# Attention with squared Relu, then a gated feed-forward block: transposes and some output tiles on all 128 rows of TensorE

## The chip, the core and the metric

The kernel runs on one core of a Trainium2 chip. The metric is the device time of one execution in microseconds (us): 432.54 before the change, the median of 7 runs (431.4 to 437.14). Inputs and output are float32 in HBM; the loads turn them to bfloat16 on the way, and all matmuls take bfloat16 and add up in float32.

## The reference

Batch 8, 12 heads, 448 tokens, 64 numbers per head. The attention has no softmax; its output, heads side by side (768 wide), goes through a gated feed-forward block with 1536 inner columns.

```python
scores = scale * np.matmul(q, k.transpose(0, 1, 3, 2))        # scale = 1/sqrt(64)
attn = np.maximum(scores, 0.0) ** 2 / S                       # S = 448
x = np.matmul(attn, v)                                        # then heads side by side: (8*448, 768)
g = x @ w_gate
gelu = 0.5 * g * (1.0 + erf(g * inv_sqrt2))
out = (gelu * (x @ w_val)) @ w_out
```

## The kernel before, in words

**Four quarters.** TensorE's array of 128 rows and 128 columns is used as four tiles of 64x64. `mm` (L158) takes a row half and a column half. A sum over 128 rows is done as two sums over 64 rows, by the lower row half (row 0) and the upper one (row 1), into the same PSUM bank. The two halves may not write a bank at the same time, so the upper half's part of a bank runs after the lower half's part: `then` (L307) puts it into the order behind it, at least 0.3 us of planned work later, and `wait_lower` (L162) makes it wait. While the upper half works on one bank, the lower half works on the next. Work whose halves write different banks runs side by side: `both` (L301).

**Stages.** A batch passes through these:
- *Transposes.* Scores need queries and keys with the 64 numbers of a head on the partitions. Queries of a chunk of 64 tokens lie on partitions 0 to 63, keys on 64 to 127 (`qk16`, 7 chunks a head). For batches 0 and 1 (`EARLY` = 2) TensorE transposes them (`add_transposes`, L319, matmuls on L333): 28 for a pair of heads, with queries on the lower and keys on the upper rows, into separate banks or halves, and VectorE copies each to `qkT` (L339). Batches 2 to 7 are transposed by DMA (`add_dma_transposes`, L248): VectorE regroups four heads (L258, into `qkr`, which has one buffer), then SP issues two transposing DMAs (L262).
- *Scores* (`add_scores`, L361): 21 units a batch. ScalarE takes the Relu out of PSUM (L387), VectorE squares it (L393).
- *Values* (`add_values`, L419): attention times v for a pair of heads; VectorE scales the bank into `xT` (L443).
- *Gate and value* (`add_gate_value`, L464): for each of 12 chunks of 128 inner columns one bank for the gate (6 steps on each row half), taken out by ScalarE as Gelu (L482), and one for the value, multiplied by VectorE into `uT` (L487).
- *Output* (`add_out`, L512): 28 tiles of 128 tokens, each in two banks of 384 columns (the last tile in three of 384, 192 and 192), 12 steps on each row half. ScalarE copies the bank to `osb` (L538); SP, at the end ScalarE too, issues the stores (L543).

PSUM has two slots for scores and transposes of batch 1 (`psS`) and a ring of four banks for the rest (`psF`).

**What sets the order.** The kernel writes every instruction in an order that a small planner (`run_plan`, L23) works out when it is built. Every piece of work gets a planned time `at` (from L561 on). The gate, value and output work of the batches stands in a row; batch 0 has output tiles 0 and 1 behind it, batch 1 has tiles 2 to 5, and so on, batch 7 tiles 23 to 27. The attention of batch 0 is placed ahead of time 0; that of batch 1 between `LO1` (L609) and 6 us before batch 1's gates start; that of later batches beside the feed-forward work of the batch before them. In planned time the gates of batch 0 take 0 to 27.2, tile 0 27.2 to 31.1, tile 1 31.1 to 35.0; batch 1's gates end at 62.2, tile 2 takes 62.2 to 66.1, and the scores of batch 2 take 41 to 71.8.

`lower`, sorted by `at`, is the fixed order of the lower rows (PE0). The upper rows' operations are sorted by the planned time of the lower operation beside which, or behind which, they belong; the planner takes from this list (PE1) the first that can start. The instruction stream of TensorE is the two merged by planned start, and it runs in that order. VectorE, ScalarE and SP take their operations in the order in which the planner finds them ready, with a planned arrival for every load; an `IDLE` operation of 2.0 us puts a regrouping behind the planned arrival of its loads. In gaps of the plan ahead of time `FILL`, `fill` (L284) puts matmuls on a zero tile.

Of the kernel before, what the change touches and what calls it, by code (L numbers as in the profile page):

```python
# [88 lines left out]
def kernel(  # L89
# [10 lines left out]
    nc = tc.nc  # L100
# [6 lines left out]
    P = 64  # L107
# [13 lines left out]
    WOG = 3  # L121
    SB = 2
    FB = 4
    FILL = 64.0
    EARLY = 2

    out_scale = 1.0 / (D * S)
# [115 lines left out]
    def by_group(t):  # L243
        return t.rearrange("d (m c r) x -> d m c r x", m=NM, c=SC)
# [3 lines left out]
    def add_dma_transposes(b, m):  # L248


        wait = Op("IDLE", 2.0, lambda: None,
                  [head_op[b, pr, i] for pr in (2 * m, 2 * m + 1) for i in range(2)])
        IDLE.append(wait)

        def emit_copy():
            if b not in qkr:
                qkr[b] = lpool.tile([128, NM, SC, 4, D], bf16, name="qkr", tag="qkr")
            nc.vector.tensor_copy(  # L258
                qkr[b][:, m], qk16[b].rearrange("p (h c d) -> p c h d", c=SC, d=D)[:, :, 4 * m:4 * m + 4])

        def emit_transpose(c0, c1):
            nc.sync.dma_start_transpose(  # L262
                by_group(qkT_tile(b))[:, m, c0:c1].rearrange("d c r x -> d (c r) x"),
                qkr[b][:, m, c0:c1].rearrange("p c h d -> p (c h d)"))

        copy = Op("DVE", 0.65, emit_copy, [wait, *tr_op.get((b - 1, m), ())], lag=0.15, prio=3)
        DVE.append(copy)
        tr_op[b, m] = [Op("SP", 0.19 * 2 * (c1 - c0), lambda c0=c0, c1=c1: emit_transpose(c0, c1),
                          [copy, last_s.get(b - 2)], lag=4.5) for c0, c1 in ((0, VC), (VC, SC))]
        SP.extend(tr_op[b, m])  # L270
# [13 lines left out]
    def fill(t0, t1):  # L284

        reader = in_bank[-FB] if len(in_bank) >= FB else None
        if reader is not None:
            if reader.end is None:
                return
            t0 = max(t0, reader.end + 0.2)  # L290
        n = int((t1 - t0 - 0.15) / 0.115)
        if t1 > FILL or n < 1:
            return
        t = new_bank(None)
        for _ in range(n):
            nc.tensor.matmul(t[:, 0:256], warm[:, 0:128], warm[:, 0:256], start=True, stop=True)  # L296

    def ring_dep():
        return [ring[-FB]] if len(ring) >= FB else []
# [19 lines left out]
    def add_transposes(at, b, m, rs):  # L319

        box = {}

        def emit(i, n, c):
            if b and not box:
                t = psS.tile([128, 2, 1024], bf16, name="sp", tag="S")
                for x in range(2):
                    box[x] = t[:, x, 0:len(rs) * SC * P].rearrange("d (r x) -> d r x", r=len(rs))
            elif i not in box:
                box[i] = new_bank(t_op[b, m, rs[0], i], [128, len(rs), SC * P], bf16)
            t = box[i]  # L330
            src = qk16[b].rearrange("p (h c d) -> p h c d", c=SC, d=D)
            for j in range(2):
                nc.tensor.transpose(  # L333
                    t[HALF[j], n, c * P:(c + 1) * P], src[HALF[i], 2 * (2 * m + rs[n]) + j, c, :],
                    ident[HALF[i], HALF[i]], tile_position=(P * i, P * j))

        def emit_copy(i):
            dst = by_group(qkT_tile(b))[:, m].rearrange("d c r x -> d r c x")
            nc.vector.tensor_copy(  # L339
                dst[:, rs[0]:rs[-1] + 1, :, HALF[i]],  # L340
                box[i].rearrange("d r (c p) -> d r c p", c=SC))

        ops = [[], []]
        for i in range(2):
            have = [*(head_op[b, 2 * m + r, i] for r in rs), *(units[-SB:1 - SB] if b else ring_dep())]
            for n in range(len(rs)):
                for c in range(SC):
                    ops[i].append(Op(f"PE{i}", 0.05, lambda i=i, n=n, c=c: emit(i, n, c),
                                     have, lag=0.2))
            t = Op("DVE", 0.07 + 0.235 * len(rs), lambda i=i: emit_copy(i),  # L350
                   [ops[i][-1], last_s.get(b - 2)], lag=0.2, prio=1)
            for r in rs:
                t_op[b, m, r, i] = t
            DVE.append(t)
            if not b:
                ring.append(t)
        if b:
            units.append(t)
        both(at, zip(*ops), GS / 2 if b else 0.0)

    def add_scores(at, b, u):  # L361


        m, w = divmod(u, SC)
        tail = w == VC - 1
        prs = (2 * m, 2 * m + 1) if tail else (2 * m + (w > VC - 1),)
        cl = w if w < VC else w - VC
        box = {}

        def emit(j, pr):  # L370
            if not box:
                box[0] = psS.tile([128, 2, 512], f32, name="sp", tag="S")
            sp = box[0]
            t = by_group(qkT_tile(b))[HALF[j], m, :, pr % 2, :]
            for i in range(2):
                if tail:
                    n0 = (pr % 2) * S // 2
                    qs = t[:, :, i * P // 2:(i + 1) * P // 2]
                    mm(sp[HALF[i], j, n0:n0 + S // 2].rearrange("k (c p) -> k c p", c=SC),
                       t[:, VC - 1, HALF[1]], qs, j, i, True, True)  # L380
                else:
                    mm(sp[HALF[i], j, 0:S].rearrange("k (c p) -> k c p", c=SC),
                       t[:, cl + i * VC, HALF[1]], t[:, :, HALF[0]], j, i, True, True)

        def emit_relu():
            rl = box[1] = rpool.tile([128, 2, S], bf16, name="rl", tag="rl")
            nc.scalar.activation(rl[:, :, :], box[0][:, :, 0:S], AF.Relu)  # L387

        def emit_sq():
            a = apool.tile([128, 2, S], bf16, name="attnT", tag="attnT")  # L390
            for pr in prs:
                att[b, pr, VC - 1 if tail else cl] = a
            nc.vector.tensor_tensor(a[:, :, :], box[1][:, :, :], box[1][:, :, :], op=ALU.mult)  # L393

        if b < EARLY:
            have = [t_op[b, m, pr % 2, i] for pr in prs for i in range(2)]
        else:
            have = tr_op[b, m]
        have = [*have, *units[-SB:1 - SB]]
        ops = [[Op(f"PE{j}", 0.095 if tail else 0.189, lambda j=j, pr=pr: emit(j, pr), have, lag=0.24)  # L400
                for pr in prs] for j in range(2)]
        last_s[b] = ops[1][-1]
        relu = Op("ACT", 0.8, emit_relu, [ops[0][-1], ops[1][-1], *sq_list[-4:-3]], lag=0.18, prio=2)
        n_a = len(sq_list)
        sq = Op("DVE", 0.54, emit_sq, [relu, *att_free[n_a - 12:n_a - 11]] if n_a >= 12 else [relu],
                lag=0.2, prio=2)
        units.append(relu)
        sq_list.append(sq)
        att_free.append(None)
        for pr in prs:  # L410
            sq_op.setdefault((b, pr), []).append((sq, n_a))
            sq_of[b, pr, VC - 1 if tail else cl] = sq
        ACT.append(relu)
        DVE.append(sq)
        both(at, zip(*ops))
# [96 lines left out]
    def add_out(at, t, g):  # L512
# [27 lines left out]
        def emit_store(j, engine, cols):  # L540
# [1 line left out]
            rows = out[b * S:(b + 1) * S, :].rearrange("(p c) d -> c p d", c=SC)  # L542
            engine.dma_start(rows[c, :, cols], osb[t][HALF[j], cols])  # L543

        ops = [[Op(f"PE{r}", step, lambda r=r, fc=fc: emit(r, fc),
                   [wo_op[fc // WOG], *(u_op[b, fc] for b, _ in chunks),
                    *(ring_dep() if r == 0 and fc == 0 else ())], lag=0.24)
                for fc in range(FC)] for r in range(2)]
        cp = Op("ACT", 0.48, emit_copy, [ops[1][-1]], prio=1)
        ring.append(cp)  # L550
        ACT.append(cp)
        if last:
# [2 lines left out]
        elif g == NG - 1:  # L555
            SP.extend(Op("SP", 0.6, lambda j=j: emit_store(j, nc.sync, slice(0, d_model)), [cp], prio=-1)
                      for j in range(2))
        then(at, step, *ops, cp)


    for h0, h1 in ((0, 2), (2, 4), (4, 8), (8, 12)):  # L561
# [44 lines left out]
            tile_no += 1  # L606
    starts.append(at)
    LEAD = 6.0
    LO1 = 2.0  # L609
    for b in range(B):  # L610
        if b == 0:
            lo, hi = -60.0, -12.0
        elif b == 1:
            lo, hi = LO1, starts[1] - LEAD
        elif b == 2:
            lo, hi = starts[1] + 6.0, starts[2] - LEAD
        else:
            lo, hi = starts[b - 1] - LEAD, starts[b] - LEAD
        step = (hi - lo) / NU
        if b < EARLY:  # L620
            for m in range(NM):
                for rs in ((0,), (1,)) if b == m == 0 else ((0, 1),):
                    work.append((lo + SC * m * step - (5.0 if b else 3.0), 1, add_transposes, (b, m, rs)))
        for pr in range(NPAIR):
            u = SC * (pr // 2) + (VC - 1, SC - 1)[pr % 2]
            work.append((lo + u * step + max(4.5, (3.2 if b == 0 else 2.5) * step), 2, add_values, (b, pr)))
        for u in range(NU):
            work.append((lo + u * step, 3, add_scores, (b, u)))
# [83 lines left out]
```

## Time and profile before

| | |
|---|---|
| median of 7 runs | 432.54 us |
| profiled execution: its time, its span | 432.57 us, 430.8 us |
| busy: TensorE, weight loads, ScalarE, VectorE, GpSimd | 419.1, 362.2, 224.7, 211.8, 71.8 us |
| transposes on TensorE (L333) | 336 of 64 columns, 5.6 to 53.9 us |
| fillers (L296) | 39 of 256 columns, the last at 28.6 us |
| regrouping (L258) | 18, 1079 ns each |
| output matmuls (`ff<-wo,uT`) | 2736 recorded, 320 ns of one on average |
| tiles 0 and 1 | 67.4 to about 80 us |
| tiles 23 to 27 | about 404.7 to 426.2 us |

A profile is one execution. The span runs from the first to the last instruction. A matmul's recorded time is from its start until its last result is out; matmuls overlap, so four in four tiles take as long as one, and the distance between starts says what a stream costs. A line of the page's groups or of the timeline gives start, length, engine, line of the kernel, operation, tile written and tiles read, shapes and count; the square brackets say how long the engine was idle before it and what released it. "SPq" and "ACTq" are the queues that issue DMAs.

### The profile page before, as it was taken

Reading aid. Unit: us, or ns where it says so; the run is one execution under the profiler, and the core shown is the slowest. Engines: PE = TensorE matmul, PEld = TensorE weight load, DVE = VectorE, ACT = ScalarE, POOL = GpSimd, SP = SyncE. Lnnn points to the kernel's source line nnn. Section 1 sums busy time; section 2 is a strip of 40 time slices with the busy share of each in tenths; the row PEclk is TensorE's granted clock in tenths of the full one; section 3 lists DMA queues with packets and bytes.
Section 4 is the critical chain, followed back from the end, with each engine's and each line's share of the span. In section 5 each row is a group of like instructions: output and inputs, shape, how many; then the busy total and the mean of one; then the engine's idle time right before and its main releaser. Section 6 shows DMA issues by size and latency. Waiting matters only on the chain.

```text
span 430.8 us, 19964 instructions
## 1 busy us (share of the span) xinstructions
PE 419.1 (97%) x9279; PEld 362.2 (84%) x9279; DVE 211.8 (49%) x345; ACT 224.7 (52%) x323; POOL 71.8 (17%) x117
## 2 busy tenths in 40 slices
PE   8999799989999999999999999999999999999995
PEld 4668599767898888979999978979999988977895
DVE  3966565357534575356633675356633555212200
ACT  3956564366566555555556555555546555322221
POOL 8655420113000230023100131012200000000000
PEclk9999999999999999999999999999999999999999
DMA  8999999999324997269914697359912100220024
GB/s 105 192 199 197 201 208 185 166 140 166 59 76 87 93 166 69 76 102 143 128 40 111 86 150 104 78 81 139 153 40 77 40 4 2 48 68 3 3 76 111
DMA packets 75378, 44.92 MB, mean 104 GB/s; under 512 B 36128, under 2 KB 71840, under 8 KB 75296
## 3 DMA queue, kind: packets, MB, share of 16 engines
q0 software_dynamic: 37088, 24.39, 42.6%
q1 hardware_dynamic: 37968, 19.08, 25.9%
q8 instruction: 72, 1.18, 1.1%
q10 hardware_dynamic: 240, 0.20, 0.2%
q14 instruction: 10, 0.08, 0.1%
HBM read 48.76 MB, written 11.01 MB: 139 GB/s over the span
## 4 chain that ended last, share of the span: by engine, by line
PE 89%; DVE 3%; SPq 2%; DMA 2%; ACT 1%; issue 1%; ACTq 0%; DVEq 0%
PE ff L159 80%; PE sp L159 7%; DMA qkT<-qkr 2%; SPq L262 2%; DVE attnT L393 1%; PE ff L676 1%; ACT rl L387 1%; DVE qkT L339 1%; PE ff L296 1%; SPq L543 1%; PE sp L333 1%; DVE xT L443 0%; ACT osb L538 0%; PE ff L333 0%; ACTq L543 0%
## 5 line engine op out<-in xcount | busy, mean ns | idle before, releaser
L159 PE MATMUL ff<-xT,wg 64*64 64x448 bf16 x2304 | 218.6, 349 | 1.9 <-issue 1.9
L159 PE MATMUL ff<-xT,wv 64*64 64x448 bf16 x2304 | 217.8, 349 | 1.4 <-DVE uT L487 1.3
L387 ACT ACTIVATE rl<-sp 128x896 bf16<-128x896 f32 x168 | 152.1, 919 | 103.1 <-PE sp L159 84.1
L159 PE MATMUL ff<-wo,uT 64*64 64x384 bf16 (+1 forms) x2736 | 151.0, 320 | 0.3 <-issue 0.3
L159 PEld LDWEIGHTS <-wv 64*64 64x64 bf16 x2304 | 126.0, 107 | 18.5 <-issue 3.4
L393 DVE TENSOR_TENSOR attnT<-rl 128x896 bf16<-128x896 bf16 x168 | 103.8, 622 | 74.6 <-ACT rl L387 73.1
L159 PEld LDWEIGHTS <-wg 64*64 64x64 bf16 x2304 | 126.2, 107 | 17.0 <-issue 3.2
L159 PEld LDWEIGHTS <-uT 64*64 64x64 bf16 x2736 | 126.5, 107 | 5.1 <-issue 0.6
L159 PE MATMUL sp<-qkT 64*64 64x448 bf16 (+1 forms) x768 | 107.4, 328 | 1.0 <-ACT rl L387 0.9
L487 DVE TENSOR_TENSOR uT<-gel,ff 128x448 bf16<-128x448 bf16 x96 | 59.5, 620 | 74.4 <-PE ff L159 63.9
L159 PE MATMUL ff<-attnT,v 64*64 64x448 bf16 (+1 forms) x768 | 85.4, 326 | 0.4 <-DVE attnT L393 0.4
L482 ACT ACTIVATE gel<-ff 128x448 bf16<-128x448 f32 x96 | 52.1, 543 | 49.2 <-PE ff L159 48.1
L538 ACT COPY osb<-ff 128x384 f32<-128x384 f32 (+1 forms) x57 | 26.9, 471 | 49.9 <-PE ff L159 46.6
L159 PEld LDWEIGHTS <-qkT 64*64 64x64 bf16 x768 | 43.7, 106 | 8.6 <-issue 3.6
L159 PEld LDWEIGHTS <-v 64*64 64x64 bf16 x768 | 45.3, 107 | 4.9 <-issue 0.6
L443 DVE TENSOR_SCALAR xT<-ff 128x448 bf16<-128x448 f32 x48 | 29.9, 623 | 32.4 <-PE ff L159 30.9
L211 POOL DMA_DIRECT2D qk<-in_q_dram x25 | 15.6, 623 | 157.2 <-DVE uT L487 148.3
L224 POOL DMA_DIRECT2D v<-in_v_dram x44 | 27.4, 629 | 34.3 <-DVE uT L487 25.6
L211 POOL DMA_DIRECT2D qk<-in_k_dram x25 | 15.4, 616 | 37.8 <-DVE uT L487 27.7
L258 DVE COPY qkr<-qk 128x1792 bf16<-128x1792 bf16 x18 | 19.3, 1079 | 3.1 <-DMA qk<-in_k_dram 3.1
L333 PEld LDWEIGHTS <-qk 64*64 64x64 bf16 x336 | 8.9, 112 | 3.9 <-issue 2.5
L333 PE MATMUL sp<-ident,qk 64*64 64x64 bf16 x168 | 6.2, 192 | 0.9 <-DVE qkT L339 0.8
(22 smaller groups left out, 44.4 us busy)
## 6 DMA issues: line engine op xcount, KB each, us to landing
out_dram<-osb SPq DMA_DIRECT2D x54, 192.0 KB, 2.7
v<-in_v_dram POOLq DMA_DIRECT2D x42, 128.0 KB, 6.1
qk<-in_q_dram POOLq DMA_DIRECT2D x23, 224.0 KB, 5.1
qk<-in_k_dram POOLq DMA_DIRECT2D x23, 224.0 KB, 5.7
wg<-in_moe_w_gate_dram POOLq DMA_DIRECT2D x6, 384.0 KB, 10.7
wv<-in_moe_w_val_dram POOLq DMA_DIRECT2D x6, 384.0 KB, 11.7
wo<-in_moe_w_out_dram POOLq DMA_DIRECT2D x4, 576.0 KB, 14.9
v<-in_v_dram POOLq DMA_DIRECT2D x2, 384.0 KB, 11.2
```

The lines of the kernel that those rows point to most:

```text
L159: return nc.tensor.matmul(o, lhsT, rhs, start=start, stop=stop, tile_position=(P * row, P * col))
L211: op = load(4 * (h1 - h0) * S * D, lambda: nc.gpsimd.dma_start(tile_of().rearrange("p (h x) -> p h x", h=H)[:, h0:h1, :], src[b, h0:h1].re ...
L224: return nc.gpsimd.dma_start(v16[b][HALF[i], h0:h1, :, :], v[b, h0:h1].rearrange("h (p c) d -> p h c d", c=SC)[:, :, c0:c0 + VC, :])
L258: nc.vector.tensor_copy(qkr[b][:, m], qk16[b].rearrange("p (h c d) -> p c h d", c=SC, d=D)[:, :, 4 * m:4 * m + 4])
L262: nc.sync.dma_start_transpose(by_group(qkT_tile(b))[:, m, c0:c1].rearrange("d c r x -> d (c r) x"), qkr[b][:, m, c0:c1].rearrange("p c h d ...
L333: nc.tensor.transpose(t[HALF[j], n, c * P:(c + 1) * P], src[HALF[i], 2 * (2 * m + rs[n]) + j, c, :], ident[HALF[i], HALF[i]], tile_positio ...
L387: nc.scalar.activation(rl[:, :, :], box[0][:, :, 0:S], AF.Relu)
L393: nc.vector.tensor_tensor(a[:, :, :], box[1][:, :, :], box[1][:, :, :], op=ALU.mult)
L443: nc.vector.tensor_scalar_mul(xT[b][:, pr, :], box[0][:, 0:S], scalar1=out_scale)
L482: nc.scalar.activation(gel[b, fc][:, :], box[0][:, 0:S], AF.Gelu)
L487: u_op[b, fc].ins = nc.vector.tensor_tensor(uT[b][:, fc, :], gel.pop((b, fc))[:, :], box[0][:, 0:S], op=ALU.mult).ins
L538: nc.scalar.copy(ob[:, cols], box[0][:, 0:N])
```

## The change

- Transposes for batches 0 and 1: one matmul transposes a chunk of queries and keys of one head together, from all 128 rows, with a 128x128 identity as the moving operand (128 columns), to one of two column halves: 14 for a pair of heads. A pair has its own bank (batch 0) or half of a slot (batch 1), one copy on VectorE, and in the plan one lower operation of 0.5 us with an empty upper one beside it.
- Planned times: `FILL` 30 instead of 64, fillers of 512 columns, batch 1's attention from 5.0 (`LO1`) instead of 2.0, other times for the transposes, and for regroupings of batches 3 to 7 an `IDLE` of 5.0 us.
- Output tiles 1, 2 and 23 to 27 ("full") are computed on all 128 rows: each of the 12 steps is two matmuls (one per column half) on 128 rows. In the plan a step is a lower operation with an empty upper one of the same cost beside it (`both`), where the other tiles keep `then`.

```diff
-    FILL = 64.0
+    FILL = 30.0
...
-        wait = Op("IDLE", 2.0, lambda: None,
+        wait = Op("IDLE", 2.0 if b == EARLY else 5.0, lambda: None,
...
-        n = int((t1 - t0 - 0.15) / 0.115)
+        n = int((t1 - t0 - 0.15) / 0.22)
...
-            nc.tensor.matmul(t[:, 0:256], warm[:, 0:128], warm[:, 0:256], start=True, stop=True)
+            nc.tensor.matmul(t[:, :], warm[:, 0:128], warm[:, :], start=True, stop=True)
...
+        def emit(r):
+            if b == 0:
+                t = new_bank(t_op[b, m, r], [128, SC, 2 * P], bf16)
+            else:
+                if not box:
+                    box["S"] = psS.tile([128, 2, 1024], bf16, name="sp", tag="S")
+                t = box["S"][:, r, 0:SC * 2 * P].rearrange("d (c x) -> d c x", c=SC)
+            box[r] = t
             src = qk16[b].rearrange("p (h c d) -> p h c d", c=SC, d=D)
...
+            for c in range(SC):
+                for j in range(2):
+                    nc.tensor.transpose(t[HALF[j], c, :], src[:, 2 * (2 * m + r) + j, c, :],
+                                        ident[:, :], tile_position=(0, P * j))
+
+        def emit_copy(r):
+            nc.vector.tensor_copy(by_group(qkT_tile(b))[:, m, :, r, :], box[r])
+
+        last = units[-SB:1 - SB]
+        for r in rs:
+            have = [*(head_op[b, 2 * m + r, i] for i in range(2)), *(last if b else ring_dep())]
+            lo = Op("PE0", 0.5, lambda r=r: emit(r), have, lag=0.2)
+            hi = Op("PE1", 0.4, lambda: None)
+            hi.after = lo
+            t = t_op[b, m, r] = Op("DVE", 0.54, lambda r=r: emit_copy(r),
+                                   [lo, last_s.get(b - 2)], lag=0.2, prio=1)
             DVE.append(t)
             if not b:
                 ring.append(t)
+            both(at, [(lo, hi)])
...
+        def emit_full(fc):
+            if not box:
+                box[0] = new_bank(cp)
+            i, o = divmod(fc, WOG)
+            for j, (b, c) in enumerate(chunks):
+                nc.tensor.matmul(box[0][HALF[j], 0:N], uT[b][:, fc, c * P:(c + 1) * P],
+                                 wo[i][:, o, cols], start=fc == 0, stop=fc == FC - 1,
+                                 tile_position=(0, P * j))
+
+
+        full = 0 < t < SC // 2 or 2 * t + 2 > SC * (B - 1) - 2
+        if full:
+            ops = [[Op("PE0", step, lambda fc=fc: emit_full(fc),
+                       [wo_op[fc // WOG], *(u_op[b, fc] for b, _ in chunks),
+                        *(ring_dep() if fc == 0 else ())], lag=0.24)
+                    for fc in range(FC)],
+                   [Op("PE1", step, lambda: None) for _ in range(FC)]]
+            for lo, hi in zip(*ops):
+                hi.after = lo
...
-        cp = Op("ACT", 0.48, emit_copy, [ops[1][-1]], prio=1)
+        cp = Op("ACT", 0.48, emit_copy, [ops[0 if full else 1][-1]], prio=1)
...
-        then(at, step, *ops, cp)
+        if full:
+            both(at, zip(*ops), step)
+        else:
+            then(at, step, *ops, cp)
...
-    LO1 = 2.0
+    LO1 = 5.0
...
-                for rs in ((0,), (1,)) if b == m == 0 else ((0, 1),):
-                    work.append((lo + SC * m * step - (5.0 if b else 3.0), 1, add_transposes, (b, m, rs)))
+                for rs in ((0,), (1,)) if b == 0 else ((0, 1),):
+
+                    x = ((0.5 if m else 1.5) * step if rs == (1,) else -4.6) if b == 0 else -5.0 if m else -2.0
+                    work.append((lo + SC * m * step + x, 1, add_transposes, (b, m, rs)))
```

More of the change, by code (lines that the diff above doesn't have):

```diff
@@ L321, in add_transposes @@
         box = {}
[L323 to L330, printed above, removed]
-            src = qk16[b].rearrange("p (h c d) -> p h c d", c=SC, d=D)
[L332 to L353, printed above, removed]
+        def emit(r):
[6 more added lines that the diff above has]
+            box[r] = t
+            src = qk16[b].rearrange("p (h c d) -> p h c d", c=SC, d=D)
+            for c in range(SC):
+                for j in range(2):
+                    nc.tensor.transpose(t[HALF[j], c, :], src[:, 2 * (2 * m + r) + j, c, :],
+                                        ident[:, :], tile_position=(0, P * j))
@@ L356, in add_transposes @@
                 ring.append(t)
+            both(at, [(lo, hi)])
         if b:
             units.append(t)
-        both(at, zip(*ops), GS / 2 if b else 0.0)
     def add_scores(at, b, u):
@@ L395, in add_scores @@
         if b < EARLY:
-            have = [t_op[b, m, pr % 2, i] for pr in prs for i in range(2)]
+            have = [t_op[b, m, pr % 2] for pr in prs]
         else:
@@ L543, in emit_store @@
             engine.dma_start(rows[c, :, cols], osb[t][HALF[j], cols])
-        ops = [[Op(f"PE{r}", step, lambda r=r, fc=fc: emit(r, fc),
+        def emit_full(fc):
[16 more added lines that the diff above has]
+        else:
+            ops = [[Op(f"PE{r}", step, lambda r=r, fc=fc: emit(r, fc),
                    [wo_op[fc // WOG], *(u_op[b, fc] for b, _ in chunks),
@@ L557, in add_out @@
                       for j in range(2))
-        then(at, step, *ops, cp)
+        if full:
+            both(at, zip(*ops), step)
+        else:
+            then(at, step, *ops, cp)
     for h0, h1 in ((0, 2), (2, 4), (4, 8), (8, 12)):
```

## The prediction

> **What bounds the kernel now.** I read the page's summary first, then the busy time by stretches, then the timeline at each stretch in which TensorE is not full, and last the chain of waits.
>
> ```profile
> PE 419.1 (97%) x9279; PEld 362.2 (84%) x9279; DVE 211.8 (49%) x345; ACT 224.7 (52%) x323; POOL 71.8 (17%) x117
> ```
>
> TensorE (PE) is busy for 97% and the others for about half. The stretches (columns: window, its length, then busy time and count for PE, weight loads, DVE, ACT, POOL) say where the other 3% and the hidden losses lie:
>
> ```profile
> 0.00:8.00 8.00, 6.81 (x89) 3.29 (x89) 1.15 (x4) 1.54 (x3) 6.95 (x18) 1.00 0.65 81
> 8.00:28.00 20.00, 18.55 (x401) 11.98 (x393) 17.88 (x33) 17.27 (x21) 12.41 (x19) 1.00 1.36 191
> ...
> 50.50:53.00 2.50, 0.56 (x20) 0.37 (x21) 0.00 (x0) 0.32 (x1) 0.61 (x1) 1.00 1.31 203
> 53.00:90.00 37.00, 36.35 (x797) 31.52 (x793) 20.34 (x32) 18.46 (x27) 5.19 (x8) 1.00 1.20 186
> 90.00:95.00 5.00, 3.71 (x80) 2.67 (x76) 2.42 (x4) 3.27 (x5) 0.61 (x1) 1.00 0.85 113
> 95.00:404.00 309.00, 309.00 (x6856) 272.94 (x6855) 154.92 (x249) 165.25 (x239) 34.27 (x56) 1.00 0.57 84
> ```
>
> From 8 to 28 us VectorE and ScalarE are full: the attention of batch 0 goes through 21 Relu evictions of about 0.83 us. At 50.5 TensorE stands for 1.94 us (in the chain, "issue"): the weights wg of the last two chunks, issued at 39.20 and 12.9 us to landing, land at about 52.1. All loads ahead of them run at 200 GB/s without a pause, so this moment is fixed. From 53 to 404 TensorE is the bound, with one hole:
>
> ```profile
> 93.21 1.09 DVE L258 COPY qkr<-qk 128x1792 bf16<-128x1792 bf16 x1 [1.98 <-DMA qk<-in_k_dram]
> ...
> 94.87 0.38 PE L159 MATMUL ff<-xT,wv 64*64 64x448 bf16 x4 [1.29 <-DVE uT L487]
> ```
>
> VectorE stands 1.98 us on the regrouping copy of batch 3, whose keys have not landed; the uT multiply behind it is late, and TensorE idles 1.29 us for its bank. The last stretch is the end:
>
> ```profile
> 423.86 2.30 PE L159 MATMUL ff<-wo,uT 64*64 64x192 bf16 x45
> ```
>
> ```profile
> 426.44 0.32 ACT L538 COPY osb<-ff 128x192 f32<-128x192 f32 x1 [0.63 <-PE ff L159]
> 426.79 0.50 ACTq L543 DMA_DIRECT2D out_dram<-osb  x1
> 427.32 0.32 ACT L538 COPY osb<-ff 128x192 f32<-128x192 f32 x1 [0.57 <-ACT osb L538]
> ```
>
> The lower rows are out of work at 423.8 and the upper rows, which trail by about one bank, run alone until 426.16. Two banks end almost together, so the last eviction waits behind its neighbour's store issue and starts 1.16 us after the last matmul.
>
> **What the Trainium skill says.** "TensorEngine Tiling (Array Packing)", Key Properties: "Changing tiling mode (not just tile) drains the TensorE". The trace of before has such changes, where a 128x128 filler stands between 64x64 matmuls:
>
> ```profile
> 12.21 0.36 PE L159 MATMUL sp<-qkT 64*64 64x448 bf16 x2
> 12.50 0.10 PEld L296 LDWEIGHTS <-warm 128*128 128x128 bf16 x1 [0.20 <-issue]
> 12.50 0.28 PE L296 MATMUL ff<-warm 128*128 128x256 bf16 x1
> 12.71 0.14 PEld L159 LDWEIGHTS <-v 64*64 64x64 bf16 x4
> 12.72 0.38 PE L159 MATMUL ff<-attnT,v 64*64 64x448 bf16 x2
> ```
>
> 448 columns take 0.187 us (pairs start 0.19 apart), so the first matmul has streamed by 12.40; the filler starts 0.10 later. It streams its 256 columns in 0.11 (fillers in a row: four in 0.61 us, (0.61-0.27)/3), to 12.61, and the next weights start 0.10 later. So the trace agrees: a change costs 0.10 us, there and back 0.20, with the exposed weight load 0.22. "TensorE: Matmul & The Clock Gate" (Part 3, The mechanism) says that a weight load overlaps a running matmul only in other row groups; the warm-up speaks against a cost here: its 20 matmuls on 128 rows take 4.48 us, so 10 pairs step by (4.48-0.63)/9 = 0.43 us, all of it the 512 columns at the cold clock, loads hidden. "PSUM — Partial Sum Buffer" (PSUM bank collisions raise a hardware error) says that row tiles may not write one bank at once: that is why the upper rows trail, and the trace shows the trail at the end.
>
> **The change part by part.** The sum is made against the profiled execution's 432.57 us (span 430.8); the median of the runs is 432.54, the same.
>
> *Transposes.* 336 of 64 columns on quarter arrays become 168 of 128 columns on half arrays. Per pair of heads: before 28 x 64/4 = 448 array columns, 0.19 us; after 14 x 128/2 = 896, 0.37 us. For the six pairs of batch 1 that is +1.1 us, and each of three blocks adds a change of mode there and back, 0.7; the evictions stay the same elements (0.62 us per 128x896). +1.8 us, at nothing, since it lies ahead of 52.1, where TensorE now stands 1.94 us for weights (and about 1 us for earlier weights at 35 to 40). Batch 0's lie under the full ScalarE. If that cover were gone, it would be +1.8. A gain here ends in the same wait.
>
> *LO1 5 instead of 2.* Of batch 1's score units, one more falls behind chunk 10 of the gates, planned at 22.68: before, 2+1.286u < 22.68 holds for u to 16; after, 5+1.143u for u to 15. One unit, +0.19 us behind the fixed moment.
>
> *FILL, coarser fillers.* The last filler runs at 28.6 us, so the limit of 30 cuts nothing; fewer fillers before it leave TensorE idle under the full ScalarE. 0; if TensorE fell back to its cold clock there, it would be part of a second, under the same cover.
>
> *Regrouping 3 us later* (batches 3 on). The copy at 93.21 goes behind about two more multiplies; the 1.98 us wait is gone and with it the idle 1.29. What is late next: two DMA transposes on SP per block, behind any output stores there, but their scores run some 20 us later; nothing. -1.3.
>
> *Full output tiles.* 7 tiles, 24 steps each, of two 384-column matmuls on 128 rows: 24 x 0.16 = 3.84 us, as many as before on four quarters; no gain in streaming. But in the plan a full step is a lower operation and an idle upper one beside it. The trailing upper operations of the bank before are merged with those idle ones one to one. So the stream reads: two full steps, one upper step alone, two full steps, one alone. Each such step costs its own 0.16 to 0.19 us, the lower rows idle, and two changes of mode, 0.22.
> - Tile 1 (now about 71 to 78 us): 12 upper steps of tile 0 and 4 of the last values of batch 1, which the plan puts inside this tile (at 32.4 of 31.1 to 35.0). Some 6 of these find a partner, 10 run alone: 10 x (0.16+0.22) = 3.8, and the lower values' own change 0.22, in all +4.0.
> - Tile 2 (about 112 us): 6 upper steps of the last value chunk, 3 score units of batch 2 and values of one pair (planned between 62.2 and 66.1). The upper halves of the scores come later than the lower ones, so 3+3 excursions, 1 for the values, some 6 alone: 13 x 0.22 = 2.9, and 9 steps alone of 0.18 = 1.6. +4.5.
> - Tiles 23 to 27: 8 upper steps are left when tile 23 starts (gates' matmuls until 405.98 beside outputs from 404.7): 8 x (0.19+0.22) = 3.3. Given back: the 2.4 us of upper rows alone at the end, and 1.1 of the last eviction, since banks now end 0.96 us apart. -0.2.
>
> Sum: +0.2 -1.3 +4.0 +4.5 -0.2 = +7.2. 432.6 + 7.2 = 439.8, say 440.
>
> The price of a change between 64 rows and 128 rows with 64 columns is not in the trace itself; the filler has 128 columns. Bounds: 0 (the rows only have to meet) to 0.15 (the first transposes start about 0.13 after the warm-up has streamed, at the cold clock). I take 0.11, as the drain is of the rows. With 0 the sum loses (10+1+13+8) x 0.22 = 7.0: +0.2.
>
> **The rivals.**
> - *Changing costs nothing* (the other side): full steps wait only for the rows they need. For it: none of the changes seen has the same 64 columns on both sides. Against it: all fillers between 64x64 matmuls show 0.2 us. Place: tiles 1, 2 and 23. It gives 432.8, no change. It decides where a round trip costs below about 0.1 us: there the sum is under +3.5.
> - *The upper rows have caught up ahead of tiles 1 and 2*: then neither is merged, the end gains 2 us and the hole 1.3: 429.3. Against it: the trail of 2.4 us at the end, which nothing shortens between.
> - *Weight loads no longer hidden* in full tiles, for want of other row groups: 7 x 24 steps with up to 0.1 us each, +17 us less half: 448 or more. Against it: the warm-up's 0.43 us.
> - *The cover ahead of 52.1 does not reach*: batch 0 ends later by over 3 us, which comes on top: 443.
>
> **How the numbers follow.** Merged steps with changes of mode 0.58 (436 to 444: a change at 0.06 to 0.15 gives +4 to +10, and some excursions more or less give the rest); changes free 0.22 (431 to 434.5); rows caught up 0.10 (428 to 431); loads exposed or cover gone 0.10. The predicted time is the likeliest's, 440. The range 431 to 444 holds the first two, 0.80, and leaves out the last two. About 1% is what a measurement of this kernel can tell from no change: slower by over 1% is 0.52 of the first and the last 0.10, 0.62; within 1% the rest of the first, the second, and half of the third, 0.33; faster 0.05.
>
> **What would show it.** Right: in the timeline of tiles 1, 2 and 23, 128x64 and 64x64 matmuls alternate, each change with 0.1 us of no start; tile 1's two banks take about 8 us instead of 4; no DVE wait on L258 at 93; the last evictions 0.96 us apart. Wrong: full and half steps following without a gap, or upper steps done ahead of the full tiles. The transposes are wrong if the wait for wg at 52 is gone; the later regrouping if the multiply still waits there.

## The result and the profile after

The changed kernel takes 442.02 us, the median of 12 runs (440.81 to 443.35); the kernel before takes 432.58 in the runs beside it. The ratio is 1.0208 (95% interval 1.0182 to 1.0235): slower by 2.1%. Some executions of one and the same kernel come out over 1.5% slower than its fastest; medians here are of all runs, ratios and their intervals of the faster runs alone. The forecast was 440.0, with 431 to 444 as its range. The profiled execution of the changed kernel took 443.35 us, the slowest of the 12 and 1.3 more than the median, and its span is 441.5, 10.7 longer than that of before.

The page's summary of the changed kernel:

```profile
PE 433.6 (98%) x8729; PEld 350.1 (79%) x8729; DVE 211.3 (48%) x343; ACT 224.5 (51%) x323; POOL 71.6 (16%) x117
```

550 matmuls fewer than before, and TensorE "busy" for 14.5 us longer. A matmul's recorded time is much longer than its streaming (0.35 us where starts lie 0.16 apart), so busy time hides short standstills: the distance between starts has to be read. Before, the matmuls of both row halves run side by side in tile 1, 26 in 1.30 us, four for every 0.16 (timeline of TensorE):

```profile
74.88 1.30 PE L159 MATMUL ff<-wo,uT 64*64 64x384 bf16 x26
```

The timeline in tile 1 of the changed kernel (tile size ahead of the operands):

```profile
72.15 0.35 PE L544 MATMUL ff<-wo,uT 128*64 128x384 bf16 x2
72.43 0.35 PE L159 MATMUL ff<-wo,uT 64*64 64x384 bf16 x2
72.71 0.35 PE L544 MATMUL ff<-wo,uT 128*64 128x384 bf16 x2
73.00 0.35 PE L159 MATMUL ff<-wo,uT 64*64 64x384 bf16 x2
```

Full steps on 128 rows (L544) and single steps of the upper 64 rows (L159) alternate, and the starts lie 0.28 to 0.29 us apart. 384 columns stream in 0.16, so 0.12 goes with each change of the row count here. The weight loads (PEld) of the same stretch start only together with their matmul:

```profile
72.43 0.11 PEld L159 LDWEIGHTS <-uT 64*64 64x64 bf16 x2 [0.17 <-issue]
72.71 0.11 PEld L544 LDWEIGHTS <-uT 128*64 128x64 bf16 x2 [0.17 <-issue]
```

Between full steps in a row the next weights are loaded while the matmul before still runs (in e4's trace 73.70 to 73.81, for a matmul at 73.86). So the price of a change may be an emptied array, a weight load that is not hidden (0.11), or both; no run here separates them.

The same stands at the seam of the last gates with tile 23, now against steps of 448 columns (0.19):

```profile
414.03 0.35 PE L544 MATMUL ff<-wo,uT 128*64 128x384 bf16 x2
414.31 0.38 PE L159 MATMUL ff<-xT,wg 64*64 64x448 bf16 x2
414.62 0.35 PE L544 MATMUL ff<-wo,uT 128*64 128x384 bf16 x2
```

0.28 from full to half, 0.31 back: 0.12 each over the streaming. At every change between 128 and 64 rows in the output tiles, the distance of the starts less the streaming of the first was summed: 34 changes at tile 1 (together 3.83 us), 22 at tile 2 (2.34), 22 at tile 23 (2.39). That is 78 changes, 8.56 us, 0.110 each on average.

The regrouping copy of batch 3, which stood 1.98 us for its load, waits for nothing any more (a line of VectorE's timeline without brackets):

```profile
99.90 1.08 DVE L258 COPY qkr<-qk 128x1792 bf16<-128x1792 bf16 x1
```

At the end the evictions of the last banks start 0.9 us apart, and the last one waits for TensorE, not for its neighbour's store (ScalarE's timeline):

```profile
437.24 0.32 ACT L532 COPY osb<-ff 128x192 f32<-128x192 f32 x1 [0.63 <-PE ff L544]
437.59 0.50 ACTq L537 DMA_DIRECT2D out_dram<-osb  x1
438.13 0.32 ACT L532 COPY osb<-ff 128x192 f32<-128x192 f32 x1 [0.57 <-PE ff L544]
```

Laying the two profiled executions side by side at the uT multiplies (each batch and chunk has one) gives where the time went, in us:

| stretch | predicted | after less before |
|---|---|---|
| to the end of batch 0's gates (transposes, FILL, LO1) | +0.2 | -0.1 |
| tile 1 | +4.0 | +5.9 |
| batch 1, chunks 3 to 6 (the hole at 93) | -1.3 | -1.4 |
| rest of batch 1's chunks | 0 | -0.2 |
| tile 2 | +4.5 | +3.9 |
| batches 2 to 7 | 0 | +1.6 |
| tiles 23 to 27 and the end | -0.2 | +1.1 |
| sum | +7.2 | +10.8 |

Each row is from one execution of either kernel. How far one execution can be trusted shows in the first row: the changed kernel and e1, e4, e5, e6, e7 and e8 below have the same plan up to tile 1, and their profiles stand there at -1.5 to +0.7 us against before (their median is -0.7); e2 and e3, with the order of before, at +0.9 and +0.5.

The 1.6 in batches 2 to 7 is mostly one stop of TensorE:

```profile
272.24 0.35 PE L159 MATMUL ff<-xT,wg 64*64 64x448 bf16 x1
...
273.78 0.35 PE L159 MATMUL ff<-xT,wg 64*64 64x448 bf16 x1 [1.18 <-issue]
```

Of a pair of gate matmuls that normally start together, the second starts 1.5 us later, released by nothing that the profile shows. The kernel before stood in this manner at 50.5 us. The third group of experiments is about it.

### The profile page after: what moved, and what is told of

It reads as the page before. It is cut to its first block, busy times and chain, and to the rows that moved or that the text cites. A ratio compares the mean times of both kernels' runs of the same rounds, so it can differ in the third digit from the quotient of the medians.

```text
span 441.5 us, 18868 instructions
## 1 busy us (share of the span) xinstructions
PE 433.6 (98%) x8729; PEld 350.1 (79%) x8729; DVE 211.3 (48%) x343; ACT 224.5 (51%) x323; POOL 71.6 (16%) x117
## 4 chain that ended last, share of the span: by engine, by line
PE 93%; DVE 3%; DMA 2%; POOL 1%; issue 1%; ACT 0%; ACTq 0%; POOLq 0%
PE ff L159 78%; PE sp L159 7%; PE ff L544 7%; DMA qk<-in_k_dram 2%; DVE attnT L387 1%; DVE xT L437 1%; PE sp L334 1%; POOL qk L211 1%; DVE qkT L338 0%; ACT osb L532 0%; PE ff L334 0%; ACTq L537 0%; PE ff L296 0%; ACT rl L381 0%; POOL ident masks.py:199 0%
## 5 line engine op out<-in xcount | busy, mean ns | idle before, releaser
L159 PE MATMUL ff<-xT,wg 64*64 64x448 bf16 x2304 | 222.8, 349 | 1.6 <-issue 1.2
L159 PE MATMUL ff<-xT,wv 64*64 64x448 bf16 x2304 | 222.7, 350 | 0.0
L159 PEld LDWEIGHTS <-wv 64*64 64x64 bf16 x2304 | 129.2, 107 | 18.9 <-issue 4.3
L159 PEld LDWEIGHTS <-wg 64*64 64x64 bf16 x2304 | 128.6, 107 | 18.8 <-issue 4.0
L159 PE MATMUL ff<-wo,uT 64*64 64x384 bf16 x2016 | 122.3, 323 | 0.0
L159 PE MATMUL sp<-qkT 64*64 64x448 bf16 (+1 forms) x768 | 108.1, 328 | 0.2
L159 PEld LDWEIGHTS <-uT 64*64 64x64 bf16 x2016 | 94.9, 107 | 10.2 <-issue 5.3
L159 PE MATMUL ff<-attnT,v 64*64 64x448 bf16 (+1 forms) x768 | 87.3, 327 | 0.1
L476 ACT ACTIVATE gel<-ff 128x448 bf16<-128x448 f32 x96 | 52.1, 543 | 62.0 <-PE ff L159 61.4
L159 PEld LDWEIGHTS <-qkT 64*64 64x64 bf16 x768 | 44.1, 106 | 10.5 <-issue 4.5
L159 PEld LDWEIGHTS <-v 64*64 64x64 bf16 x768 | 46.1, 107 | 6.5 <-issue 1.7
L544 PE MATMUL ff<-wo,uT 128*64 128x384 bf16 (+1 forms) x360 | 34.8, 321 | 0.0
L544 PEld LDWEIGHTS <-uT 128*64 128x64 bf16 x360 | 17.7, 109 | 12.9 <-issue 8.0
```

The lines of the kernel that those rows point to most:

```text
L159: return nc.tensor.matmul(o, lhsT, rhs, start=start, stop=stop, tile_position=(P * row, P * col))
L476: nc.scalar.activation(gel[b, fc][:, :], box[0][:, 0:S], AF.Gelu)
L544: nc.tensor.matmul(box[0][HALF[j], 0:N], uT[b][:, fc, c * P:(c + 1) * P], wo[i][:, o, cols], start=fc == 0, stop=fc == FC - 1, tile_positi ...
```

## The experiments

Theory A is the prediction's sum: each change of the row count costs about 0.11 us, and the trailing upper steps, merged one by one with the full steps, make many of them. Theory B is its rival: changes are free, and what time is lost comes from rows that idle and from other things that the rebuilt order moves. For the stop at 50 us, theory W is the prediction's (TensorE waits for weights, wg); against it stands that TensorE runs out of instructions. Ratios are against the kernel before, in runs beside each kernel.

**Which part costs the time: e1, e2, e7.** e1 is the changed kernel without full tiles:

```diff
-        full = 0 < t < SC // 2 or 2 * t + 2 > SC * (B - 1) - 2
+        full = False
```

> The changed kernel with no full output tile: all tiles on four quarters again; transposes, regrouping and planned times as changed. Theory A (changes between 64-row and 128-row matmuls, two of 0.11 us for each upper step that stands alone among full steps) and theory B (only the lower rows' idleness beside those steps) both put the whole loss into the full tiles: 431 us, since the batch of gates after the transposes ends 0.3 earlier than before and the hole at 93 us (1.3) is gone. Rival C (the transposes on 128 rows or the later start of batch 1 cost time): 434 or more.

Measured: 431.44 us (20 runs), ratio 0.9976 [0.9954, 0.9997], span 428.9. That is what A and B have; rival C falls. e2 is the other half: the kernel before with only the hunk of the output tiles.

> The kernel before with nothing changed but output tiles 1, 2 and 23 to 27 on all 128 rows. A and B: 441 to 443: the same 76 changes of mode and upper steps alone; the hole at 93 us should close by itself, since TensorE comes later than VectorE's wait. C: 438 or less. Also expected: the stop of about 2 us at 50.5 us, which the changed kernel does not have, is here again, at the same place in the order, because the order up to there is that of the kernel before.

Measured: 443.14, ratio 1.0248 [1.0182, 1.0314], span 440.8; 76 changes of the row count in the output tiles. e7 keeps only the full tiles at the end:

```diff
-        full = 0 < t < SC // 2 or 2 * t + 2 > SC * (B - 1) - 2
+        full = 2 * t + 2 > SC * (B - 1) - 2
```

> The changed kernel with full tiles only at the end (23 to 27), none at 1 and 2. 22 changes of mode are left. A: 2.4 us for these and 1.7 for 10 upper steps alone, less 2.4 of upper rows alone at the end and 1.1 of the last eviction: 0.6 to 1.1 us over the kernel without full tiles, about 432. B: 1.5 to 2 us under the kernel without full tiles, about 429.

Measured: 433.18 (12 runs), ratio 0.9994 [0.9965, 1.0024], 1.7 over e1; 22 changes with 2.38 us. The whole loss lies in the full tiles, most of it in tiles 1 and 2 (442.02 - 433.18 = 8.8), and even those at the end cost 1.7, nearer to A's forecast than to B's. e7 alone doesn't say what in them costs: rows that idle would cost too.

**What in the full tiles costs: e4, e5, e6.** e4 keeps every full tile and takes away only the alternation. A full bank waits in the plan for the last three upper operations of the banks before it, and its steps stand together:

```diff
+            ops[0][0].deps += last_upper
...
-            both(at, zip(*ops), step)
+            both(at, zip(*ops), 0.0)
...
-            hi[0].after = PE0[behind]
+            hi[0].after = lo if PE0[behind].full else PE0[behind]
```

`last_upper` is kept in `then`; an upper operation whose place would be beside a full step goes right behind its own lower one instead. 10 changes border full tiles instead of 78.

> The changed kernel, but each bank of a full tile waits in the plan until the upper rows have done what they trail by, and its 12 full steps stand together. 10 changes of mode border full tiles instead of 78; the upper steps still run with the lower rows idle. A: 68 changes of 0.11 us fewer, 7.5 us: 434.5 us. B: no gain, 441 to 443, as the upper steps are alone as before.

Measured: 434.28 (20 runs), ratio 1.0033 [1.0016, 1.0051], span 432.4. TensorE's timeline of e4 in tile 1:

```profile
73.52 2.14 PE L547 MATMUL ff<-wo,uT 128*64 128x384 bf16 x24
75.59 1.76 PE L160 MATMUL ff<-attnT,v 64*64 64x448 bf16 x16
77.28 2.14 PE L547 MATMUL ff<-wo,uT 128*64 128x384 bf16 x24
79.35 0.38 PE L160 MATMUL ff<-xT,wg 64*64 64x448 bf16 x2
```

A bank's 24 matmuls run in one piece; from its start to the next work are 2.07 us, less one change of 0.12 that is 12 steps of 0.16. The same matmuls are issued as in the changed kernel, with 68 changes fewer, and 7.74 us are gone: 0.114 each, if the new order changed nothing else. Under B e4 would not have moved so much. What is left against e1 (2.84 us) would be ten changes (1.1) and rows that idle: at the uT multiplies of the two profiled executions e4 loses 2.9 us to e1 in tile 1, 2.65 in tile 2, and gains 1.2 at the end.

Gathering steps also moves other work about, so e5 and e6 measure the price by itself. Both put two matmuls of 64 columns on zero data, into an unread slot, after every third step of the full tiles 24 to 27, 36 pairs in all. In e5 they are on 64 rows:

```diff
+            if t > 23 and fc % 3 == 1:
...
+                mm(sc[HALF[0], 0, 0:P], warm[HALF[0], 0:P], warm[HALF[0], 0:P], 0, 0, True, True)
+                mm(sc[HALF[1], 0, 0:P], warm[HALF[0], 0:P], warm[HALF[0], 0:P], 0, 1, True, True)
```

> The changed kernel with 36 pairs of small matmuls (64 columns, zero data, into a PSUM slot nobody reads) on 64 rows, put between full steps of tiles 24 to 27: 72 more changes of mode than in its twin on 128 rows. Theory A (0.11 us a change): 7.9 us over the twin. Theory B (a change is free): within 1 us of the twin. Over the changed kernel: A 9 us, 451; B about 1 us, 443.

In e6 the same two are on 128 rows, so nothing changes:

```diff
+                for j in range(2):
+                    nc.tensor.matmul(sc[HALF[j], 0, 0:P], warm[:, 0:P], warm[:, 0:P], start=True, stop=True,
+                                     tile_position=(0, P * j))
```

> The twin: the same 36 pairs of small matmuls on 128 rows with 64 columns, in the mode of the full tiles, so no change of mode is added. A and B: 36 x 0.03 us, 443 us; if a small matmul on 128 rows waits for its weight load (about 0.1 us), 446.

Measured: e5 450.95, ratio 1.0397 [1.0347, 1.0448]; e6 444.46, ratio 1.0228 [1.0168, 1.0288]. TensorE's timeline of e5 and, below it, of e6:

```profile
430.21 0.22 PE L159 MATMUL sp<-warm 64*64 64x64 bf16 x2
430.36 0.68 PE L546 MATMUL ff<-wo,uT 128*64 128x384 bf16 x6
430.97 0.22 PE L159 MATMUL sp<-warm 64*64 64x64 bf16 x2
```

```profile
430.43 0.20 PE L554 MATMUL sp<-warm 128*64 128x64 bf16 x2
430.45 0.66 PE L546 MATMUL ff<-wo,uT 128*64 128x384 bf16 x6
430.94 0.20 PE L554 MATMUL sp<-warm 128*64 128x64 bf16 x2
```

Three full steps with a small pair take 0.76 us on 64 rows and 0.51 on 128: two changes are 0.25. Over the whole end, from the first eviction of tile 23 to the last of all, e5 takes 29.34 us and e6 20.86: 8.5 us for 72 changes, 0.118 each. The medians (4 runs each) differ by 6.5, 0.09 each. Up to tile 24 the two kernels have the same instructions, and yet in the profiled executions e5 reached tile 23 2.3 us sooner; so the stretch is the better measure. The 36 small pairs themselves cost little: e6's end takes 1.1 us longer than that of the changed kernel (19.78), 0.03 for a pair, as forecast. B falls here for good: data and columns are the same in both, and the rows that idle in e5 alone do so only during the 36 small pairs, about 1 us in all.

**The best of both: e8.** e4's gathering with e7's choice of tiles, so that full tiles stand only at the end, with 2 changes.

> The changed kernel with full tiles only at the end (23 to 27), and there only after the upper rows have done what they trail by: 2 changes of mode border full tiles. Theory A (a change of mode costs 0.11 us): in the kernel with all full tiles gathered the end, from tile 23 on, took 1.3 us less than before; on top of the kernel without full tiles (431.4) that gives 430.1. Theory B (full tiles cost for their idle rows, changes or not): 433, as with full tiles at the end merged with upper steps.

Measured: 430.43 (16 runs), ratio 0.9923 [0.99, 0.9947], span 429.8. That is A's forecast. It beats the kernel before by 0.8% and e1 by 1.0 us between medians (the two were not run side by side, but the intervals of their ratios don't meet). A full tile at the end does pay, once the trailing steps are out of its way.

**The rest: e3, e10, e9.** e3 is the kernel before with only the later regrouping:

```diff
-        wait = Op("IDLE", 2.0, lambda: None,
+        wait = Op("IDLE", 2.0 if b == EARLY else 5.0, lambda: None,
```

> The kernel before with the later regrouping of batches 3 to 7 alone. Theory R (VectorE's wait on the copy of L258 at 93 us holds up the multiply and TensorE): the wait and TensorE's 1.29 us hole are gone, 431.3 us; the stop at 50.5 us stays. Rival: the loads and the last transposing DMA land at 92.8 anyway and something else waits for them, no change within 0.4 us.

Measured: 432.09 (22 runs), ratio 0.9985 [0.9968, 1.0003]. In its trace the wait is gone and the first multiply behind it comes 2.2 us sooner, later ones 1.4, but the runs show a gain of 0.15% whose interval includes none: theory R's 431.3 did not come. The likely reason is the load, whose landing differs from one execution to the next: in the profiled execution of before, batch 3's keys landed at 92.85 us; in those of e3, e9 and e10 at 90.99, 91.67 and 91.78, in that of e1 at 92.72. e9 and e10 keep the old regrouping, and yet they too gain 1.5 and 1.3 us on before between chunks 3 and 6. VectorE waits only this long there (VectorE's timeline of e10):

```profile
91.96 1.08 DVE L258 COPY qkr<-qk 128x1792 bf16<-128x1792 bf16 x1 [0.65 <-DMA qk<-in_k_dram]
```

e10 is the changed kernel with only its transposes: no full tiles, `IDLE` 2.0, `LO1` 2.0, `FILL` 64.

> The kernel before with the transposes on 128 rows alone and their own planned offsets: LO1, the limit for fillers and the regrouping wait as before, no full tile. Theory F: halving the transposes' instructions takes the stop at 50.5 us away (1.9), their doubled array time and changes of mode take about 1.8 back: 432 to 432.8, and the hole at 93 us is there. Rival W: the stop stays and the doubled array time is hidden ahead of it: also 432.6, but with TensorE standing at 50 to 52.

Measured: 432.76 (22 runs), ratio 0.9984 [0.9965, 1.0003]. The stop at 50 us was gone, as in the changed kernel and in e1; TensorE's hole at 93 that was expected was not there: VectorE had waited 0.65 us, not 1.98. e9 leaves the transposes as before but cuts the last block of 56 of batch 1 in two, the second half 3 us later in the plan:

```diff
-                for rs in ((0,), (1,)) if b == m == 0 else ((0, 1),):
-                    work.append((lo + SC * m * step - (5.0 if b else 3.0), 1, add_transposes, (b, m, rs)))
+                for rs in ((0,), (1,)) if b == m == 0 or (b, m) == (1, 2) else ((0, 1),):
+                    work.append((lo + SC * m * step - (5.0 if b else 3.0) + (3.0 if b and rs == (1,) else 0.0), 1, add_transposes, (b, m, rs)))
```

> The kernel before, but the last block of 56 transposes of batch 1 (planned at 15.0) is cut into two of 28, the second 3 us later. Theory F (the stop of 1.94 us at 50.5 us is TensorE out of instructions, after a stretch of 152 in 2 us where 43 in 1 us are usual): the stop is gone or under 0.5 us, batch 0's last multiply comes 1.5 us earlier or more, and the end is at 431 to 432.5, part of it given back in the wait at 93 us. Rival W (the stop waits for weights that land at 52, as the prediction had it): TensorE stands until 52 as before, and the last multiply of batch 0 does not come earlier.

Measured: 432.33 (22 runs), ratio 0.9991 [0.9971, 1.001], span 431.1. The stop of 1.94 us is gone, but TensorE now waits 0.51 and 0.46 us for VectorE's copies to `qkT`, until 49.42 and 51.42, and batch 0's last multiply comes only 0.37 us sooner than in before, not 1.5 as expected. So e9 alone doesn't decide against W. The other traces do: in before, e2 and e3 the stop is 1.94 us long each time, though the weights it was said to wait for landed 0.42, 0.98 and 0.79 us ahead of its end; in the changed kernel they landed at 52.17, and TensorE has no stop of 0.1 us between 40 and 60 us. Nor does e9 keep what it gains: it stands 0.65 us at 58, 1.14 at 76.9 and 1.05 at 309.6, where before has only 0.26 at 76.4. TensorE's timeline of e9 at the second of them:

```profile
76.88 0.36 PE L159 MATMUL ff<-wo,uT 64*64 64x384 bf16 x4 [1.14 <-issue]
```

What these stops have in common is in the DMA view, which lists the core's own fetches of instructions as a queue. Of before between 49.9 and 51.0 us, and of e9 between 73.9 and 74.9 (queue, kind, then packets, MB, share of 16 engines):

```profile
q8 instruction: 1, 0.02, 5.4%
```

```profile
q8 instruction: 1, 0.02, 6.0%
```

One packet of 16 KB in each; in before it ran from 50.00 to 50.95, and TensorE went on at 52.48. And the stretches of before ahead of the stop (window, length, then busy time and count of PE and of weight loads first):

```profile
45.00:46.00 1.00, 1.00 (x26) 0.84 (x21) 1.00 (x2) 0.85 (x1) 0.79 (x2) 1.00 1.47 196
48.00:49.00 1.00, 1.00 (x50) 0.91 (x47) 0.68 (x2) 0.29 (x2) 0.64 (x1) 1.00 1.45 196
49.00:50.00 1.00, 1.00 (x44) 0.88 (x38) 0.93 (x3) 0.68 (x1) 0.30 (x1) 1.00 1.46 198
```

The 56 short transposes double the number of instructions in a microsecond; by their starts 152 matmuls and weight loads fall into 48 to 50 us, where about 43 a microsecond are usual. (The view counts at the edges what reaches over them twice.) In the changed kernel the last transposes of batch 1, half as many, run from 50.67 to 51.76:

```profile
51.00:52.00 1.00, 1.00 (x30) 0.71 (x28) 0.56 (x1) 0.34 (x1) 0.11 (x1) 1.00 1.38 204
```

30 and 28 in place of 50 and 47, and no stop follows. After 40 us, in all eleven changed kernels and before, every stop of 0.2 us or more whose next matmul waits for no semaphore (14 in all) ends 1.3 to 2.0 us after the end of such a fetch; a fetch comes about every 5.8 us, so chance would put few of them there. That TensorE had run out of instructions fits this, but it is argued, not shown: no run took away a fetch alone. Nor does a burst alone explain the stops: in before, the 177 matmuls and weight loads in the two microseconds from 34.9 are followed by no such stop, and the 11 stops that are not those at 50 us have only 62 to 80 in the two microseconds ahead of them.

## Why the prediction was right, and where it was not

The kernel is slower for the reason that was forecast, and the forecast was low: +7.2 us against +9.4 between the medians. It came that near partly by luck, since errors of both signs met.

**Price of a change: right.** Taken as 0.11 us from the fillers, it is 0.110 on average over the 78 changes of the changed kernel (0.117 for most from 64 to 128 rows, 0.096 or 0.120 for most on the way back), 0.114 by e4 and 0.118 by e5 against e6. The Trainium skill, "TensorEngine Tiling (Array Packing)", Key Properties, says that a change of tiling mode drains TensorE; all these runs agree that a change costs time and put a number to it, also where both tiles have 64 columns. How much of it is the drain and how much a weight load that is not hidden, they don't show. The rival of free changes is refuted.

**Merged steps: right in kind, mis-sized in number.** The alternation in tiles 1, 2 and 23 stands in the trace as forecast. The sum had 11, 13 and 8 round trips; there are 17, 11 and 11, 39 instead of 32. At tile 1 too many of the 16 upper steps were taken to find a partner, 6 of them: 17 round trips cost 3.8, and the 2.1 that is left is about the streaming of the steps that ran alone (13 of output tiles at 0.16 and 2 of values), so +5.9 stands where +4.0 was predicted. Tile 2 has two fewer: +3.9 where +4.5 was. At the end the three extra round trips and their own streaming eat up what the missing trail gives back: +1.1 where -0.2 was. The error of the three terms together is +2.6 us, and it lies in the count of pairs, which was made in planned time; what shifted them was not looked at.

**The cover at 52.1: the step that failed.** The prediction put the transposes at nothing because "the weights wg of the last two chunks" hold TensorE until about 52.1, "so this moment is fixed". They don't: the matmuls at the stop are those of chunk 7's gate and chunk 6's value, whose weights had landed at 42.1 and 44.1; the late weights belong to chunks 10 and 11, and chunk 10 runs at about 63 us. The stop was gone in every kernel in which the block of transposes was halved or cut, with these weights landing at 50.8 to 52.2 us as ever. Nor does TensorE stand "about 1 us for earlier weights at 35 to 40": it stands 0.41 us there for a copy to `qkT` on VectorE, and 0.10 without a cause in the profile. The prediction took the landing that lay nearest for the cause, in a wait for which the chain said "issue", without asking which chunk the next matmul belongs to. The term came out near right all the same (-0.1 at the end of batch 0's gates, against +0.2), which is luck: seven executions with this plan spread from -1.5 to +0.7 there. What is in it is a balance that was not foreseen, no stop of 1.94 us against more array time and changes, the latter put at 1.8 and not measured by itself.

**Regrouping: right in this pair of traces, not in general.** The -1.3 is there as -1.4, but e3 shows that between medians it is 0.6 us or nothing. The wait of 1.98 us was that of one execution, in which the keys landed over a microsecond later than in e3, e9 and e10; in e1 they landed as late. How often they do is not known.

**Not foreseen:** the stop at 272 us, 1.2 of the 10.8. It isn't fixed to the program: e6, whose instructions up to tile 24 are the changed kernel's, shows it with 0.65 us at 273, and e5, with the same instructions up to there, shows none of 0.2 us. The trace of before could not have told the place.

**Other rivals.** Rows caught up: no, the trailing steps are in the trace. Loads exposed: no, full steps follow each other at 0.16 us, the pace of their streaming, and load their weights beside a running matmul on the same rows (e4); what the prediction cites on weight loads and row groups did not bind here. Its own argument, the warm-up's 0.43 us for 512 columns, left this open, since at the pace of later matmuls (0.16 for 384) they would take 0.21; the trace settles it, for the warm-up's loads end 0.25 us ahead of their matmul (3.51 and 3.75 us). Why the first 5 us run at half the later pace no run here shows. Cover gone: the cover was never there, and what the rival added (3 us) did not come.

## What to carry to other kernels

A change of the tile's row count cost TensorE 0.11 to 0.12 us each time here, so count the changes in the merged order, not the tiles: before a piece of work on other rows, let what trails finish, and run the piece as one block. Idle "issue" time without a semaphore is no wait for data until the instruction next in line has been shown to need that data. And a wait on a load in one execution may not be there in the next: look at the landing time in a second trace before counting on it.

## What the runs showed of the hardware that was not expected

TensorE can stand although nothing that the profile shows holds it. After 152 matmuls and weight loads in 2 us it stopped for 1.94 us in before, and for the same time in e2 (to 51.84) and e3 (to 51.79); the stop is gone in every kernel in which that block of transposes was halved or cut. But 177 of them in 2 us, at 35 us in before, brought no such stop, and stops of up to 1.18 us came elsewhere after no more than 80. A fetch of 16 KB on the instruction queue took 0.95 us there, and TensorE resumed 1.3 to 2.0 us after the end of one each time. That the fetch is the cause stays open.
